# Unsplit float32 second products for every second chunk of block 1 in an attention and two-layer MoE kernel

## The chip, the core and the metric

The kernel runs on one core of one Trainium2 chip. The metric is the device time of one execution in microseconds (us). Engines are named as in the profile: PE is TensorE, PEld its weight loads, DVE is VectorE, ACT is ScalarE, POOL is GpSimd, SP is SyncE.

## What is computed

Attention over 1536 tokens (2 batches of 768, 8 heads of 64) with a window and block sums, then a dense feed-forward layer, then a layer of 8 experts with one expert per token. The change is in the dense layer, with 1536 tokens, a width of 512 and a hidden width of 2048:

```python
def _moe_ref(x, w_in, w_out):
    h = x @ w_in
    g = np.where(h > 0.0, h, np.exp(np.minimum(h, 0.0)) - 1.0)
    return (g @ w_out).astype(np.float32)

# reference: x = attention(q, k, v); x = _moe_ref(x, ...); return _moe2_ref(x, ...)
```

`g @ w_out` is called the second product here.

## The kernel before

The tokens are handled in four blocks of 512, 256, 384 and 384 tokens (`UNITS` = 8, 4, 6, 6 units of 64); block 1 is the second one, with two tiles of 128 tokens. The hidden width is cut into 16 chunks of 128. The first part of the program, `part1`, goes through 64 steps (block j, chunk c). In step i it issues, in this order: `mm_h` (the first product of chunk c, 12 matmuls into a PSUM bank h, of which there are two), `split_w` for the same chunk, `split_g` for the chunk of the step before, `elu` (three ACT operations, L432 to L434, and two DVE operations, L435 and L436, which leave g in the tile elp), and `mm_y` for the chunk of two steps before, which adds into the block's banks y, one for each tile of 128 tokens. Beside these, the steps carry the attention of the later blocks (`scores` L308, `turn` L370, `weighted` L391 and what belongs to them), and, in the first steps of a block, the logits of the block before (`lg1` and `lg2`, L499 to L525).

Full float32 precision is reached in two ways. Split: a float32 number is cut into a high part in the type fp32r and the remainder, and a product is made of three matmuls (high with high, high with low, low with high). For the second product this takes two operations for the weights of a chunk (`split_w`: an ACT cast at L174 and a DVE subtraction at L175, into the tile wsp) and two for g (`split_g`: L446 on ACT into gh, L447 on DVE into gl). Unsplit: one matmul instruction on the float32 tiles as they are, with weights straight from the tile wo and g from elp. Before the change the first eight chunks of block 0 are unsplit (`C3` = 8).

elp of a split chunk lies in a pool of two buffers with the tag p. gh and gl have two buffers each; an unsplit chunk of block 0 puts its elp into one of theirs, odd chunks under the tag gh, even ones under gl.

The order on each engine in `part1` is not that of the code: a scheduler with a timeline of its own places the instructions, except in the start-up, whose order is a hand-written table. The second part (routing of the last block and the experts) is ordered by a planner with fixed costs; it contains no second product of block 1.

Of the kernel before, what the change touches and what calls it, by code (L numbers as in the profile page):

```python
# [35 lines left out]
BLK = [j for j in range(NBLK) for _ in range(UNITS[j])]  # L36
NF = FF // 128
NS = 6
C3 = 8
WARM = 22  # L40
AT0 = (2, -2, 1)
ATS = (5, 4, 5)
# [36 lines left out]
class Prog:  # L79
# [86 lines left out]
            self.conv_l(c)  # L166

    def split_w(self, j, c):
        if j == 0 and c < C3:
            return  # L170
        nc = self.nc
        f = self.w[c, 1].bitcast(F32)
        w = self.ws.tile([128, 2, 512], F32R, tag="ws", name="wsp")
        nc.scalar.copy(w[:, 0], f)  # L174
        nc.vector.tensor_tensor(w[:, 1], f, w[:, 0].bitcast(F32), op=ALU.subtract)  # L175
        self.wsp[j, c] = w
# [247 lines left out]
    def elu(self, j, c):  # L424
        nc = self.nc
        h = self.h.pop((j, c))
        t = self.el.tile([128, TB], F32, tag="t", name="elt", bufs=1)[:, :TBS[j]]
        e = self.el.tile([128, TB], F32, tag="e", name="ele", bufs=1)[:, :TBS[j]]

        pool, tag = (self.gp, "gh" if c % 2 else "gl") if j == 0 and c < C3 else (self.el, "p")  # L430
        p = pool.tile([128, TB], F32, tag=tag, name="elp")[:, :TBS[j]]
        nc.scalar.activation(t, h, AF.Tanh, scale=0.5)  # L432
        nc.scalar.activation(e, h, AF.Exp)  # L433
        nc.scalar.activation(p, h, AF.Relu)  # L434
        nc.vector.scalar_tensor_tensor(t, e, 1.0, t, op0=ALU.add, op1=ALU.mult)  # L435
        nc.vector.scalar_tensor_tensor(p, t, 0.0, p, op0=ALU.min, op1=ALU.add)  # L436
        self.g[j, c] = p

    def split_g(self, j, c):
        nc = self.nc  # L440
        if j == 0 and c < C3:
            return
        p = self.g[j, c]
        gh = self.gp.tile([128, TB], F32R, tag="gh", name="gh")[:, :TBS[j]]
        gl = self.gp.tile([128, TB], F32R, tag="gl", name="gl")[:, :TBS[j]]
        nc.scalar.copy(gh, p)  # L446
        nc.vector.tensor_tensor(gl, p, gh.bitcast(F32), op=ALU.subtract)  # L447
        self.g[j, c] = (gh, gl)
# [7 lines left out]
    def mm_y1(self, j, c, t):  # L456
        nc = self.nc
        g = self.g[j, c]
        sl = slice(t * 128, t * 128 + 128)
        if j == 0 and c < C3:  # L460
            ops = ((g, self.w[c, 1].bitcast(F32)),)
        else:
            w = self.wsp[j, c]
            ops = ((g[0], w[:, 0]), (g[0], w[:, 1]), (g[1], w[:, 0]))
        for n, (gx, wx) in enumerate(ops):
            nc.tensor.matmul(self.y[j][t], lhsT=gx[:, sl], rhs=wx, start=(c == 0 and n == 0), stop=(c == NF - 1 and n == len(ops) - 1))  # L466
# [1032 lines left out]
```

## Time and profile before

| | |
|---|---|
| median of 3 runs | 552.49 us (551.38 to 555.17) |
| the profiled execution | 552.2 us, span of its instructions 550.4 us |
| PE busy | 528.4 us (96% of the span) |
| DVE, ACT, POOL busy | 357.8, 312.5, 74.2 us |
| mean granted clock of TensorE | 0.994 of full speed |

The profile is one execution. Busy times are shares of the span. Matmuls are pipelined, so the duration of a single one contains its drain; how much work PE gets through is read from the distance between the starts of consecutive matmuls.

### The profile page before, as it was taken

The numbers are of one execution on the slowest core, as the hardware profiler recorded it, in microseconds if no ns is written. First come the engines' busy times: TensorE is split into PE (matmuls) and PEld (weight loads), VectorE is DVE, ScalarE is ACT, GpSimd is POOL, SyncE is SP. The second block draws the span as 40 slices with busy tenths as digits, with TensorE's granted clock in tenths as the row PEclk, the third lists the DMA queues.
The fourth block names the chain that finished last, engine by engine and source line by source line (L and its number), as shares of the span: only waits on it lengthen the run. The fifth ranks groups of instructions, "written<-read, shape, count | busy, mean of one in ns | idle before, by whom it ended". The sixth has DMA issues, their size and how long they took to land. (4 is left out here: it accounts for less than half of the span.)

```text
span 550.4 us, 9589 instructions
## 1 busy us (share of the span) xinstructions
PE 528.4 (96%) x3113; PEld 417.6 (76%) x3113; DVE 357.8 (65%) x994; ACT 312.5 (57%) x768; POOL 74.2 (13%) x111
## 2 busy tenths in 40 slices
PE   7867999999998999999999999999999999999995
PEld 4456666688897888988888888978888575575883
DVE  6999899999557887786565789986631101444510
ACT  5875567767458786776665756662233232565620
POOL 3653000001000000000000001421421111100001
PEclk9999999999999999999999999999999999999998
DMA  9999843433114112211001004431286979594601
GB/s 296 315 359 403 269 155 105 151 99 95 53 56 153 49 50 80 69 49 49 2 0 59 1 1 130 120 96 57 67 299 243 393 255 358 156 381 140 236 21 42
DMA packets 38715, 81.34 MB, mean 148 GB/s; under 512 B 4095, under 2 KB 8575, under 8 KB 38656
## 3 DMA queue, kind: packets, MB, share of 16 engines
q1 hardware_dynamic: 36336, 73.30, 39.4%
q0 software_dynamic: 2320, 7.34, 3.8%
q8 instruction: 26, 0.43, 0.3%
q14 instruction: 33, 0.27, 0.1%
HBM read 103.70 MB, written 6.55 MB: 200 GB/s over the span
## 5 line engine op out<-in xcount | busy, mean ns | idle before, releaser
L421 PE MATMUL h<-xh,wi 128*128 128x384 f32 (+2 forms) x528 | 145.9, 343 | 0.5 <-ACT elp L434 0.5
L421 PEld LDWEIGHTS h<-xh,wi 128*128 128x128 f32 x528 | 94.0, 189 | 8.6 <-issue 1.0
L466 PE MATMUL y<-wsp,gh 128*128 128x512 f32 x320 | 98.5, 398 | 0.1
L421 PE MATMUL h<-xl,wi 128*128 128x384 f32 (+2 forms) x264 | 87.9, 333 | 0.0
L466 PEld LDWEIGHTS y<-wsp,gh 128*128 128x128 f32 x320 | 57.8, 188 | 10.1 <-ACT gh L446 0.6
L1157 DVE TENSOR_TENSOR holdl<-S,holdh 128x512 fp32r<-128x512 f32 x22 | 15.2, 689 | 72.5 <-ACT holdh L1153 53.7
L466 PE MATMUL y<-wsp,gl 128*128 128x512 f32 x160 | 60.5, 399 | 0.0
L1125 PE MATMUL h<-w2s,holdh 128*128 128x512 f32 x176 | 59.8, 400 | 0.0
L1168 PE MATMUL y<-w2s,holdh 128*128 128x512 f32 x176 | 59.0, 398 | 0.0
L421 PEld LDWEIGHTS h<-xl,wi 128*128 128x128 f32 x264 | 49.8, 189 | 4.6 <-issue 1.4
L435 DVE SCALAR_TENSOR_TENSOR elt<-ele,elt 128x384 f32<-128x384 f32 (+2 forms) x64 | 37.1, 580 | 23.8 <-ACT ele L433 23.5
L432 ACT ACTIVATE elt<-h 128x384 f32<-128x384 f32 (+2 forms) x64 | 31.3, 489 | 36.2 <-PE h L421 30.1
L175 DVE TENSOR_TENSOR wsp<-wo,wsp 128x512 fp32r<-128x512 f32 x56 | 39.2, 703 | 8.5 <-ACT wsp L174 8.0
L174 ACT CAST wsp<-wo 128x512 fp32r<-128x512 f32 x56 | 34.6, 621 | 15.6 <-PE y L466 13.1
L446 ACT CAST gh<-elp 128x384 fp32r<-128x384 f32 (+2 forms) x56 | 27.8, 497 | 21.8 <-DVE elp L436 14.7
L1168 PEld LDWEIGHTS y<-w2s,holdh 128*128 128x128 f32 x176 | 33.1, 188 | 8.4 <-issue 1.6
L1125 PEld LDWEIGHTS h<-w2s,holdh 128*128 128x128 f32 x176 | 33.1, 188 | 8.1 <-issue 0.8
L436 DVE SCALAR_TENSOR_TENSOR elp<-elt,elp 128x384 f32<-128x384 f32 (+2 forms) x64 | 35.5, 554 | 3.2
L335 ACT ACTIVATE e<-e,nb 128x120 f32<-128x120 f32 x88 | 33.7, 390 | 6.4 <-DVE nb L323 6.3
L447 DVE TENSOR_TENSOR gl<-elp,gh 128x384 fp32r<-128x384 f32 (+2 forms) x56 | 31.1, 555 | 7.6 <-ACT gh L446 7.6
L296 POOL COPY k<-ks 128x96 f32<-128x96 f32 x16 | 8.2, 516 | 199.3 <-PE S L308 137.6
L1168 PE MATMUL y<-w2s,holdl 128*128 128x512 f32 x88 | 34.4, 391 | 0.0
(291 smaller groups left out, 949.7 us busy)
## 6 DMA issues: line engine op xcount, KB each, us to landing
wo<-in_w SPq DMA_DIRECT2D x9, 2048.0 KB
wo<-in_w SPq DMA_DIRECT2D x18, 1024.0 KB
ri<-in_w_in SPq DMA_DIRECT2D x16, 512.0 KB
ro<-in_w_out SPq DMA_DIRECT2D x16, 512.0 KB
wo<-in_w SPq DMA_DIRECT2D x32, 256.0 KB
w2p<-in_w SPq DMA_DIRECT2D x32, 256.0 KB
w2q<-in_w SPq DMA_DIRECT2D x24, 256.0 KB
q<-in_q SPq DMA_DIRECT2D x18, 256.0 KB
```

The source lines that it names most:

```text
L174: nc.scalar.copy(w[:, 0], f)
L175: nc.vector.tensor_tensor(w[:, 1], f, w[:, 0].bitcast(F32), op=ALU.subtract)
L335: nc.scalar.activation(e[:, p], e[:, p], AF.Exp, bias=nb[:, p:p + 1], scale=0.125, accum_out=sm[:, p:p + 1])
L421: nc.tensor.matmul(h, lhsT=w[:, wl, k * 128:k * 128 + 128], rhs=x[:, k, a:b], start=(n == 0), stop=(n == 11))
L432: nc.scalar.activation(t, h, AF.Tanh, scale=0.5)
L435: nc.vector.scalar_tensor_tensor(t, e, 1.0, t, op0=ALU.add, op1=ALU.mult)
L436: nc.vector.scalar_tensor_tensor(p, t, 0.0, p, op0=ALU.min, op1=ALU.add)
L446: nc.scalar.copy(gh, p)
L447: nc.vector.tensor_tensor(gl, p, gh.bitcast(F32), op=ALU.subtract)
L466: nc.tensor.matmul(self.y[j][t], lhsT=gx[:, sl], rhs=wx, start=(c == 0 and n == 0), stop=(c == NF - 1 and n == len(ops) - 1))
L1125: nc.tensor.matmul(self.h[s, hf], lhsT=x[:, k], rhs=w, start=(n == 0), stop=(n == 11))
L1168: nc.tensor.matmul(self.y2[s], lhsT=g[:, ks], rhs=w, start=(i == 0 and n == 0), stop=(i == 7 and n == 2))
```

## The change

A set `WHOLE` of pairs (block, chunk) replaces the constant `C3`. It holds chunks 0 to 7 of block 0, as before, and the even chunks 0, 2, ... 14 of block 1. For these, `split_w` and `split_g` do nothing, `mm_y1` issues one float32 matmul for each tile in place of three, and `elu` puts elp into a buffer of gh or gl; in block 1 chunks 0, 4, 8 and 12 take gl, and 2, 6, 10 and 14 take gh.

```diff
-C3 = 8
+WHOLE = {(0, c) for c in range(8)} | {(1, c) for c in range(0, NF, 2)}
@@ split_w
-        if j == 0 and c < C3:
+        if (j, c) in WHOLE:
             return
@@ elu
-        pool, tag = (self.gp, "gh" if c % 2 else "gl") if j == 0 and c < C3 else (self.el, "p")
+        pool, tag = (self.gp, "gh" if (c >> j) % 2 else "gl") if (j, c) in WHOLE else (self.el, "p")
@@ split_g
-        if j == 0 and c < C3:
+        if (j, c) in WHOLE:
             return
@@ mm_y1
-        if j == 0 and c < C3:
+        if (j, c) in WHOLE:
             ops = ((g, self.w[c, 1].bitcast(F32)),)
```

The scheduler places everything around it anew. Three places show how. First PE where block 1's second products begin, right behind the first matmuls of block 0's logits (L524, on mab). y<-wsp,gh and y<-wsp,gl are split passes, y<-wo,elp is an unsplit product, "x2" is two instructions in a row. Before:

```order
L499 MATMUL y<-c_128,m 128x128 x4
L466 MATMUL y<-wsp,gh 128x512 x2
L466 MATMUL y<-wsp,gl 128x512
L466 MATMUL y<-wsp,gh 128x512 x2
L466 MATMUL y<-wsp,gl 128x512
L370 MATMUL T<-c_128,e 120x128 x4
L466 MATMUL y<-wsp,gh 128x512 x2
L466 MATMUL y<-wsp,gl 128x512
L466 MATMUL y<-wsp,gh 128x512 x2
L466 MATMUL y<-wsp,gl 128x512
L524 LDWEIGHTS mab
```

and in the change, at the same place:

```order
L499 MATMUL y<-c_128,m 128x128 x4
L466 MATMUL y<-wo,elp 128x512
L466 MATMUL y<-wsp,gh 128x512 x2
L466 MATMUL y<-wsp,gl 128x512
L466 MATMUL y<-wo,elp 128x512
L370 MATMUL T<-c_128,e 120x128 x4
L466 MATMUL y<-wo,elp 128x512
L466 MATMUL y<-wsp,gh 128x512 x2
L466 MATMUL y<-wsp,gl 128x512
L466 MATMUL y<-wo,elp 128x512
L524 LDWEIGHTS mab
```

Before, chunks 0 and 1 of one tile, then of the other, stand here; now chunks 0, 1 and 2 do, with 0 and 2 unsplit.

Second, PE in the middle of the block, at the end of the first product of chunk 10 (weights wi_1151) and the beginning of that of chunk 11 (wi_1200); between them stands the second product of chunk 8. Before:

```order
L391 MATMUL T<-et,v_98 64x64 x8
L308 MATMUL S<-k,q 128x120 x4
L421 MATMUL h<-xh_203,wi_1151 128x256
L421 MATMUL h<-xl_204,wi_1151 128x256
L421 MATMUL h<-xh_203,wi_1151 128x256
L466 MATMUL y<-wsp,gh 128x512 x2
L466 MATMUL y<-wsp,gl 128x512
L466 MATMUL y<-wsp,gh 128x512 x2
L466 MATMUL y<-wsp,gl 128x512
L421 MATMUL h<-xh_203,wi_1200 128x256
```

and in the change:

```order
L391 MATMUL T<-et,v_98 64x64 x8
L308 MATMUL S<-k,q 128x120 x4
L421 MATMUL h<-xh_203,wi_1151 128x256 x2
L421 MATMUL h<-xl_204,wi_1151 128x256
L421 MATMUL h<-xh_203,wi_1151 128x256
L466 MATMUL y<-wo,elp 128x512 x2
L421 MATMUL h<-xh_203,wi_1200 128x256
```

Six passes have become two instructions; the chunk's place, two steps behind its first product, is the same.

Third, ACT at the beginning of block 1, from the activations of chunk 0 to those of chunk 2. Before:

```order
L434 ACTIVATE elp<-h 128x256
L174 CAST wsp<-wo 128x512
L446 CAST gh<-elp 128x256
L236 COPY vs<-T 128x4x4
L432 ACTIVATE elt<-h 128x256
L433 ACTIVATE ele<-h 128x256
L434 ACTIVATE elp<-h 128x256
L236 COPY vs<-T 128x4x4
L446 CAST gh<-elp 128x256
L174 CAST wsp<-wo 128x512
L432 ACTIVATE elt<-h 128x256
```

and in the change:

```order
L434 ACTIVATE elp<-h 128x256
L174 CAST wsp<-wo 128x512
L236 COPY vs<-T 128x4x4
L432 ACTIVATE elt<-h 128x256
L433 ACTIVATE ele<-h 128x256
L434 ACTIVATE elp<-h 128x256
L446 CAST gh<-elp 128x256
L236 COPY vs<-T 128x4x4
L174 CAST wsp<-wo 128x512
L432 ACTIVATE elt<-h 128x256
```

The cast gh of chunk 0 is gone, and that of chunk 1 stands one place earlier. The orders of all engines are the same up to this place, but for names, and again from the middle of block 2 on.

## Rows read from the trace of the kernel before

**Rows 1.** Page, busy us of PE, and the granted clock in 40 slices

```profile
PE 528.4 (96%) x3113; PEld 417.6 (76%) x3113; DVE 357.8 (65%) x994; ACT 312.5 (57%) x768; POOL 74.2 (13%) x111
...
PEclk9999999999999999999999999999999999999998
```

**Rows 2.** Busy time by stretch; block 1 is 148.50:218.50

```profile
core 0: us, PE busy (x) PEld busy (x) DVE busy (x) ACT busy (x) POOL busy (x), PEclk, DMA share, GB/s
60.00:107.00 47.00, 47.00 (x216) 29.53 (x214) 42.96 (x107) 31.86 (x76) 0.27 (x1) 1.00 0.49 167
...
148.50:218.50 70.00, 68.62 (x556) 61.14 (x555) 51.38 (x181) 50.75 (x158) 2.20 (x7) 1.00 0.23 73
218.50:300.00 81.50, 81.50 (x531) 72.54 (x531) 54.62 (x161) 53.53 (x142) 1.08 (x3) 1.00 0.11 34
...
460.00:500.00 40.00, 40.00 (x194) 25.52 (x192) 16.28 (x26) 21.35 (x39) 4.41 (x4) 1.00 0.76 264
500.00:550.40 50.40, 43.60 (x204) 34.37 (x200) 13.13 (x21) 17.04 (x30) 4.91 (x5) 0.97 0.31 109
```

**Rows 3.** Timeline, ACT and PE around the wait: start us, us, engine, what

```profile
162.44 0.59 ACT L377 COPY et<-T 120x512 f32<-120x512 f32 x1 [0.93 <-PE T L370]
...
166.66 0.63 ACT L511 CAST mab<-y 128x512 bf16<-128x512 f32 x1
...
167.34 0.20 PE L524 MATMUL y<-wg,mab 128*128 128x48 bf16 x1 [1.38 <-ACT mab L511]
```

**Rows 4.** Groups by line, 148.5:218.5, DVE and ACT: busy us, mean ns, idle before

```profile
L175 DVE TENSOR_TENSOR wsp<-wo,wsp 128x512 fp32r<-128x512 f32 x16 | 11.0, 688 | 1.9 <-ACT wsp L174 1.7
L447 DVE TENSOR_TENSOR gl<-elp,gh 128x256 fp32r<-128x256 f32 x16 | 6.8, 426 | 2.2 <-ACT gh L446 2.2
...
L174 ACT CAST wsp<-wo 128x512 fp32r<-128x512 f32 x17 | 10.5, 620 | 4.2 <-PE y L466 4.2
...
L446 ACT CAST gh<-elp 128x256 fp32r<-128x256 f32 x16 | 6.5, 404 | 1.0 <-DVE elp L436 0.5 <-PE y L466 0.4
```

**Rows 5.** Groups by line and form, whole span, PE: all second products

```profile
L466 PE MATMUL y<-wsp,gh 128*128 128x512 f32 x320 | 98.5, 398 | 0.1
...
L466 PE MATMUL y<-wsp,gl 128*128 128x512 f32 x160 | 60.5, 399 | 0.0
...
L466 PE MATMUL y<-wo,elp 128*128 128x512 f32 x64 | 30.9, 622 | 2.5 <-DVE elp L436 2.5
```

**Rows 6.** Timeline, PE, an unsplit chunk of block 0

```profile
67.87 3.59 PE L466 MATMUL y<-wo,elp 128*128 128x512 f32 x8
70.90 0.79 PE L421 MATMUL h<-xh,wi 128*128 128x512 f32 x1
71.53 0.39 PE L421 MATMUL h<-xl,wi 128*128 128x512 f32 x1
```

**Rows 7.** Timeline, PE, two split chunks of block 1

```profile
196.03 0.63 PE L466 MATMUL y<-wsp,gh 128*128 128x512 f32 x2
...
197.41 0.28 PE L421 MATMUL h<-xh,wi 128*128 128x256 f32 x1
...
198.84 1.09 PE L466 MATMUL y<-wsp,gh 128*128 128x512 f32 x4
...
200.23 0.60 PE L370 MATMUL T<-c,e 128*120 128x128 f32 x4
```

**Rows 8.** Timeline, PE, from transposes back to split passes

```profile
200.59 0.37 PE L421 MATMUL h<-xh,wi 128*128 128x256 f32 x1
200.79 0.28 PE L421 MATMUL h<-xl,wi 128*128 128x256 f32 x1
200.91 0.40 PE L421 MATMUL h<-xh,wi 128*128 128x256 f32 x2
```

**Rows 9.** Timeline, ACT and PE at the beginning of block 1

```profile
149.48 0.39 ACT L434 ACTIVATE elp<-h 128x256 f32<-128x256 f32 x1
...
150.42 0.82 PE L308 MATMUL S<-k,q 128*128 128x120 f32 x6
...
152.07 0.17 ACT L236 COPY vs<-T 128x16 f32<-128x16 f32 x1 [0.53 <-PE T L235]
```

**Rows 10.** Timeline, chunk 1 of block 1, from h to elp

```profile
153.29 0.28 PE L421 MATMUL h<-xh,wi 128*128 128x256 f32 x1
...
154.83 0.43 DVE L436 SCALAR_TENSOR_TENSOR elp<-elt,elp 128x256 f32<-128x256 f32 x1
```

## The prediction, made before the changed kernel ran

> **What bounds the kernel now.** I read the busy shares first: TensorE (PE) is busy for 528.4 of 550.4 us, and its granted clock is at the upper level (2.4 GHz) in nearly every slice [rows 1]. An average says nothing about one stage, so the second view is busy time by stretch. Block 1, the one that the change touches, occupies PE from about 148.5 to 218.5 us. There PE is busy for 68.62 of 70.00 us, VectorE (DVE) for 51.38 and ScalarE (ACT) for 50.75 [rows 2]. So PE is the limit of this stage and the other two have over 18 us of slack each. The missing 1.38 us is one single wait of PE, for the part mab of block 0's logits, which ACT makes late [rows 3].
>
> Next comes what follows. From 218.5 to 300 us PE is busy for 81.50 of 81.50 us, from 460 to 500 us for 40.00 of 40.00 [rows 2]; only the tail after 500 us has larger holes. Whatever PE gains or loses in block 1 is therefore handed on: the work behind it already stands in an unbroken queue on PE. DVE and ACT time is worth something only where PE waits for it.
>
> **The removed work that is not on the path.** Eight chunks (c = 0, 2, ... 14) lose four instructions each: the two halves of the split of w_out (L174 on ACT, 0.620 us, L175 on DVE, 0.688 us) and the two of the split of g (L446 on ACT, 0.404 us, L447 on DVE, 0.426 us) [rows 4]. That is 8 x 1.024 = 8.2 us of ACT and 8 x 1.114 = 8.9 us of DVE. I cost all of it at nothing for the end time: both engines were idle for 18 us in this stretch, and PE waited for them 1.38 us in total. That is also the upper bound of what this relief can pay directly.
>
> Is even that 1.38 us freed? The wait ends with the ACT cast that starts at 166.66 us [rows 3]. In the order above, ACT's rows before that cast are those of before apart from one gh cast gone and a few casts moved, all of them before 160 us, and after them ACT runs dry: it waits 0.93 us for PE's transposes before the copy at 162.44 [rows 3]. What stands between that copy and the cast (copies of y, exponentials, xh) is unchanged. So the wait stays; I take 0 and keep -1.4 us as the end of the range.
>
> **The work on the path.** A split product of one 128-token tile is three PE passes (gh with w high, gh with w low, gl with w high). The unsplit product replaces these three by one instruction, which looks like a third of the work. The trace shows that it isn't. Block 0 already does c = 0 to 7 that way: 8 chunks x 4 tiles = 32 products, but the row on elp counts 64 matmuls [rows 5]. One float32 instruction is two records. In the timeline, eight such records start at 67.87 and the second matmul behind them starts at 71.53 [rows 6]. The first of those behind them takes one ordinary pass of 0.23 us, so the eight end at 71.53 - 0.23 = 71.30: 3.43 us, 0.43 us for a record and **0.858 us for a product**. The 0.59 us that rows show as a duration contains pipeline drain and must not be used.
>
> For the split form I read starts of consecutive work in block 1: a chunk's two tiles run from 196.03 to 197.41 us and another's from 198.84 to 200.23 us [rows 7], 1.38 and 1.39 us for six passes. That is 0.23 us a pass and **0.692 us for a product**. So each of the 16 products (8 chunks x 2 tiles) becomes 0.166 us longer: 16 x 0.166 = **+2.6 us on PE**.
>
> Weight loads add nothing of their own: they are inside these start-to-start distances in both forms. As the upper bound I keep the busy time of all 64 records, 30.9 us [rows 5], over 32 products: 0.966 us, drain and the first, slow batch included; that would be 16 x 0.274 = +4.4 us.
>
> The Trainium skill ("FP8 and Floating Point Precision", section "TensorE Precision Notes") says that true FP32 makes four passes through the array. With the trace's 0.23 us a pass that would be 0.92 us, and the sum +3.7 instead of +2.6 us; the trace's 0.858 us is a little under it and decides.
>
> **What the new order changes.** Where PE goes from a float32 transpose or score product to a split pass, it loses about 0.08 us: after the transposes, the matmul that starts at 200.59 is followed only at 200.79, 0.20 us later, where its neighbours follow at 0.12 us [rows 8]. Counted in the order of both kernels from the first score product of block 1 to the first h of block 2, such places (into a split or an unsplit matmul) fall from 17 to 14: 3 x 0.08 = -0.2 us. What the way back from a float32 product into split passes costs is already inside the 0.858 us, since [rows 6] is read past that switch. The remaining moves in block 2 exchange neighbours among work that was ready anyway; 0, with 0.3 us either way.
>
> **The waits that the buffers add.** elp of a whole chunk now lives in a buffer of tag gl or gh, so its Relu (L434) has to wait until an older part there has been read. In steady state that reader is the y product of three chunks earlier, which stands on PE ahead of the chunk's own h, so there is no wait. The start is different: chunk 0's elp takes the gl buffer of block 0's chunk 14, whose last pass ends as the next product starts at 150.42 us, while before its Relu began at 149.48 [rows 9]. ACT is held for about 1 us. Queued behind it stand one weight cast and the copy of vs, and that copy sat idle for 0.53 us until 152.07 anyway [rows 9]. Chunk 0's g is not read until after 167 us [rows 3]. Cost on PE: 0; bound above, 0.5 us, if the copy moved by the rest.
>
> **The sum.** +2.6 - 0.2 = +2.4 us. The profiled execution took 552.2 us with a span of 550.4, so it would become 554.6. The median of the runs shown is 552.49 us, 0.3 above the profiled one; I forecast **554.9 us**, a ratio of 1.004. About 1% (5.5 us) is what a measurement of this kernel can tell from no change, so this is a small loss inside that bound.
>
> **Rivals.**
> 1. *The relief pays after all.* The wait of 1.38 us goes, and block 1 loses most of its 17 switches. At most 2.6 - 1.4 - 17 x 0.08 = -0.2 us, so 552.3; the likely form (the wait alone) is 2.4 - 1.4 = +1.0, so 553.5. For it: 17 us of work leave the two engines. Against: the queue ahead of the cast is unchanged and PE has no other hole.
> 2. *The float32 product is as cheap as it looks:* one record of 0.43 us for a product. 16 x (0.43 - 0.692) = -4.2, so 548.3 us, faster than before. Against it stands the count of 64 records for 32 products, so I give it next to nothing.
> 3. *PE waits for elp.* The y product of a whole chunk now depends on Relu and two DVE operations directly. In chunk 1 of before, h ends at about 153.5 (last matmul at 153.29) and elp is ready at 154.83 + 0.43 = 155.26 us [rows 10], a chain of 1.8 us. What covers it: the order puts y(c-2), h(c+1), y(c-1) and h(c+2) between h(c) and y(c), 1.72 + 1.43 + 1.39 + 1.43 = 6.0 us (h from 197.41 to 198.84 in [rows 7]). It decides only if ACT's queue stretches the chain past 6.0 us; if it came to 7 us in all eight chunks, 8 x 1.0 us join: 562.9. Against it: block 0, with the same form, keeps PE busy for 47.00 of 47.00 us from 60 to 107 us [rows 2].
>
> **How the numbers follow.** Forecast 0.74, rival 1 0.13, rival 2 0.02, rival 3 0.07, and 0.04 for what I can't name, on both sides. The likeliest gives the time, 554.9. Below, the range takes rival 1's end, 552.3, and the 1.1 us by which the fastest run shown lies under the median (551.2), and above the upper bound of the product with one more wait of the size of the old one: 552.5 + 4.4 + 1.4 = 558.3, so 558.4. Faster by over 1% (under 547.0) is rival 2 with a lucky order: 0.03. Slower by over 1% (over 558.0) is rival 3 and a part of the unnamed: 0.10. The rest, 0.87, lies within 1%.
>
> **What would show it.** Right: the elp row of L466 counts 96 matmuls, gh 288 and gl 144; eight short stretches of block 1 with two products take 1.72 us each, start to start, against 1.39; the stretch from chunk 0's h to block 2's first h is about 72.4 instead of 70 us; busy PE rises by some 2.4 us while ACT falls by 8 and DVE by 9; the wait for mab is still there with 1.4 us; later stretches are the old ones, shifted. Wrong: a record count of 80 for elp (rival 2); a vanished mab wait (rival 1); idle time ahead of L466 rows with releaser L436 (rival 3); or PE holes behind 220 us that the table of stretches did not have.

## The result, and the profile after

| | before | after |
|---|---|---|
| median, timed side by side | 552.8 us (551.09 to 556.6) | 556.49 us (554.81 to 558.07) |
| profiled execution, span | 552.2, 550.4 us | 554.81, 553.0 us |

The ratio is 1.006, with a 95% interval of 1.0043 to 1.0077: the change costs 2.4 to 4.3 us. The forecast was 554.9 us, a ratio of 1.004, with 0.87 on "within 1%". The size, the sign and the place held; the forecast lies at the low end of the interval. It took about 1% as the least that can be told from no change; with 20 runs on each side the interval is 0.17% to either side, so this loss is told apart from none. Ratios, here and below, are of means, over the runs that lie at most 1.5% above the fastest of their kernel.

First the page after, the row that answers to [rows 1]:

```profile
PE 531.5 (96%) x3097; PEld 414.9 (75%) x3097; DVE 349.4 (63%) x978; ACT 306.4 (55%) x752; POOL 73.2 (13%) x111
```

PE gained 3.1 us of busy time while DVE lost 8.4 and ACT 6.1 (the rows of ACT that are gone lasted 8.2 us in all, but rows that follow each other overlap, and busy time counts an overlap once). Work left the two engines that had time and came to the one that had none.

The groups of the second product over the whole span, which answer to [rows 5] (busy us, mean ns | idle before):

```profile
L466 PE MATMUL y<-wsp,gh 128*128 128x512 f32 x288 | 90.8, 402 | 0.0
...
L466 PE MATMUL y<-wsp,gl 128*128 128x512 f32 x144 | 54.9, 398 | 0.0
...
L466 PE MATMUL y<-wo,elp 128*128 128x512 f32 x96 | 44.8, 594 | 2.5 <-DVE elp L436 2.5
```

16 products more without a split are 32 records more of elp (64 to 96), 32 fewer of gh and 16 fewer of gl. So a float32 matmul is two records in block 1 as well. And the only wait of all these rows for L436 is the old one of 2.5 us at the start of block 0.

Next the timeline of PE at one unsplit chunk of block 1, and at the logits (the second answers to [rows 3]):

```profile
178.34 1.88 PE L466 MATMUL y<-wo,elp 128*128 128x512 f32 x4
180.06 0.38 PE L370 MATMUL T<-c,e 128*120 128x128 f32 x2
```

```profile
166.58 0.20 PE L524 MATMUL y<-wg,mab 128*128 128x48 bf16 x1 [1.38 <-ACT mab L511]
```

Two products take 180.06 - 178.34 = 1.72 us, where the split form took 1.38 and 1.39 [rows 7]: 0.17 us more for each. The wait for mab has not changed by a hundredth.

Busy time by stretch, with the same columns as [rows 2]:

```profile
148.50:221.20 72.70, 71.32 (x541) 58.41 (x540) 46.21 (x168) 44.98 (x143) 1.60 (x6) 1.00 0.23 72
...
221.20:300.00 78.80, 78.80 (x516) 69.53 (x515) 51.92 (x156) 50.71 (x137) 0.95 (x3) 1.00 0.10 31
```

PE's only hole is still those 1.38 us, and behind block 1 it has none.

Where did the time go? One execution can't be compared by its span, because the clock differs in other places (last section). Two places of the program mark the stretch in which the orders differ: the transposes of vs at the beginning of block 1, and the first transposes of m in block 3 (from there on the orders are equal again). Before:

```profile
159.11 0.60 PE L242 MATMUL T<-c,vs 128*24 128x128 f32 x4
...
302.02 0.60 PE L499 MATMUL T<-c,m 128*128 128x128 f32 x4
```

After:

```profile
158.35 0.60 PE L242 MATMUL T<-c,vs 128*24 128x128 f32 x4
...
303.97 0.60 PE L499 MATMUL T<-c,m 128*128 128x128 f32 x4
```

That is 142.91 us before and 145.62 after: **+2.71 us**, against +2.4 in the forecast's sum. This distance, at an undisturbed clock of 1.00 and with the same work inside but for the second products that the edit changes, is the measure for the experiments on blocks 1 and 2 below; I call it the marked stretch.

### The profile page after: what moved, and what is told of

Read it like the earlier page. It is cut to its first block, busy times and chain, and to the rows that moved or that the text cites. A ratio compares the mean times of both kernels' runs of the same rounds, so it can differ in the third digit from the quotient of the medians.

```text
span 553.0 us, 9537 instructions
## 1 busy us (share of the span) xinstructions
PE 531.5 (96%) x3097; PEld 414.9 (75%) x3097; DVE 349.4 (63%) x978; ACT 306.4 (55%) x752; POOL 73.2 (13%) x111
## 5 line engine op out<-in xcount | busy, mean ns | idle before, releaser
L466 PE MATMUL y<-wsp,gh 128*128 128x512 f32 x288 | 90.8, 402 | 0.0
L1157 DVE TENSOR_TENSOR holdl<-S,holdh 128x512 fp32r<-128x512 f32 x22 | 15.2, 690 | 72.4 <-ACT holdh L1153 53.7
L466 PEld LDWEIGHTS y<-wsp,gh 128*128 128x128 f32 x288 | 52.3, 188 | 10.2 <-issue 1.4
L466 PE MATMUL y<-wsp,gl 128*128 128x512 f32 x144 | 54.9, 398 | 0.0
L466 PE MATMUL y<-wo,elp 128*128 128x512 f32 x96 | 44.8, 594 | 2.5 <-DVE elp L436 2.5
L175 DVE TENSOR_TENSOR wsp<-wo,wsp 128x512 fp32r<-128x512 f32 x48 | 33.7, 706 | 8.4 <-ACT wsp L174 7.9
L436 DVE SCALAR_TENSOR_TENSOR elp<-elt,elp 128x384 f32<-128x384 f32 (+2 forms) x64 | 35.5, 555 | 4.4 <-ACT elp L434 0.9
L174 ACT CAST wsp<-wo 128x512 fp32r<-128x512 f32 x48 | 29.6, 621 | 15.5 <-PE y L466 14.6
L446 ACT CAST gh<-elp 128x384 fp32r<-128x384 f32 (+2 forms) x48 | 24.6, 512 | 23.0 <-DVE elp L436 14.4
L1125 PE MATMUL h<-w2s,holdl 128*128 128x512 f32 x88 | 35.0, 398 | 0.0
```

The lines of the kernel that those rows point to most:

```text
L1125: nc.tensor.matmul(self.h[s, hf], lhsT=x[:, k], rhs=w, start=(n == 0), stop=(n == 11))
L1157: self.nc.vector.tensor_tensor(l, self.tx.pop((s, hf)), h.bitcast(F32), op=ALU.subtract)
```

## Experiments: how much for a product, and does the place matter

Four theories were to be told apart. A: a price for each product on PE. B: a loss from the new order or the buffers, whatever the number. C: the relief of ACT and DVE pays a part back. D, which came up on the way: in other places the work that a split product puts on ACT and DVE is what counts. The recorded expectations use letters of their own, explained in each of them, which don't always agree with these.

**All chunks of block 1 unsplit**, 32 products instead of 16:

```diff
-WHOLE = {(0, c) for c in range(8)} | {(1, c) for c in range(0, NF, 2)}
+WHOLE = {(j, c) for j, n in ((0, 8), (1, NF)) for c in range(n)}
```

> All 16 chunks of block 1 are unsplit, 32 products in place of 16, elp alternating between the buffers of gl and gh as in block 0. Theory A (only the length of the products on PE counts, 0.166 us each): +5.3 us less about 0.3 us of switches, about 557.8 us where before has 552.8, ratio 1.009. Theory B (the work taken off ScalarE and VectorE pays too, so that the loss flattens): twice the work is taken off, no wait for mab, ratio 1.006 or less. Theory C (each unsplit product costs what the end-to-end result says, 3.3 us over 16, because of something beside its length): +6.6 us, ratio 1.012. In the profile A shows the mab wait still there with about 1.4 us.

Measured: 556.96 us, ratio 1.0067 (1.0043 to 1.0091); the marked stretch is 4.18 us longer than before, so the second 16 products cost 1.47 us, about half of the first 16. The wait for mab is still there with 1.4 us, so it isn't the end of this wait that flattens the loss.

**A quarter of the chunks**, 0, 4, 8 and 12, with elp in a buffer of its own: 8 products.

```diff
+WHOLE = {(0, c) for c in range(8)} | {(1, c) for c in range(0, NF, 4)}
+        if j == 1 and c % 4 == 0:
+            p = self.el.tile([128, TBS[1]], F32, tag="pw", name="elp", bufs=1)
```

> Half the dose: only chunks 0, 4, 8 and 12 of block 1 are unsplit, 8 products in place of 16, and their elp lie in a buffer of their own. Theory A (a price per product on PE, 0.166 us): 8 x 0.166 = +1.3 us, ratio to the kernel before 1.0024; from the transposes of vs at the start of block 1 to block 3's first transposes of m the profile is 1.3 us longer (the change: +2.71, all 16 chunks: +4.18). Theory B (most of the loss is a fixed one, from the new order, whatever the number of products): about +2.7 us, 1.005. Theory C (the relief of ACT and DVE pays and is worth more the less PE has to bear): at or below 1.000.

Measured: 554.67 us, ratio 1.002 (0.9998 to 1.0042), which by itself can't be told from no change; the marked stretch is 1.03 us longer.

**Another place**: block 1 split again, and five chunks of block 2 with three tiles each unsplit, 15 products.

```diff
+WHOLE = {(0, c) for c in range(8)} | {(2, c) for c in range(1, NF, 3)}
```

> The same form in another place: block 1 all split as before, and in block 2 chunks 1, 4, 7, 10 and 13 unsplit, 5 chunks x 3 tiles = 15 products, their elp again in the buffers of gh and gl. Theory A (a price per product, wherever it stands): 15 x 0.166 = +2.5 us, ratio 1.0045. Rival (the loss belongs to block 1, to its start beside the logits of block 0 and the buffers there): 1.000 to 1.002 here.

Measured: 556.64 us, ratio 1.0063 (1.0041 to 1.0085). The two marks in this kernel, and the next transposes of m:

```profile
160.15 0.60 PE L242 MATMUL T<-c,vs 128*24 128x128 f32 x4
...
305.18 0.60 PE L499 MATMUL T<-c,m 128*128 128x128 f32 x4
...
310.08 0.60 PE L499 MATMUL T<-c,m 128*128 128x128 f32 x4
```

To the first transposes of m it is 2.12 us longer than before. But here these stand two matmuls of h earlier than in the other kernels, so the stretch holds less work. Up to the second transposes the work is the same again but for the 15 products; before, these were at

```profile
306.58 0.60 PE L499 MATMUL T<-c,m 128*128 128x128 f32 x4
```

That is 149.93 us against 147.47: 2.46 us longer.

| unsplit products more | 8 | 15 (block 2) | 16 (the change) | 32 |
|---|---|---|---|---|
| marked stretch, us longer | 1.03 | 2.46 (to the second transposes of m) | 2.71 | 4.18 |
| for a product | 0.13 | 0.16 | 0.17 | 0.13 |
| ratio | 1.002 | 1.0063 | 1.006 | 1.0067 |

The loss grows with the number of products and is there in block 2 as well. Theory B, a fixed loss that belongs to block 1, falls. The price in the stretch is 0.13 to 0.17 us. Two products in a row took 1.72 us in the kernel with 32 too, so their price is the same, and the other work of the stretch takes less time there. Fewer changes between kinds of matmul (37 places with 32 products, 41 before) explain 0.3 of the 1.1 us by which 32 products missed 32 x 0.166 = 5.3. Most of the rest is seen in `weighted` (L391): before, its matmuls stand in 16 runs, with 32 products in 13, and from the start of each run to the next work it is 8.19 us in all before and 7.53 with 32. A run cut in two is dearer than a whole one, here 0.61 + 0.26 us (before) against 0.61 (32 products):

```profile
171.45 0.68 PE L391 MATMUL T<-et,v 120*64 120x64 f32 x14
172.06 0.20 PE L524 MATMUL y<-wg,mab 128*128 128x48 bf16 x1
172.19 0.33 PE L391 MATMUL T<-et,v 120*64 120x64 f32 x2
172.45 1.21 PE L466 MATMUL y<-wsp,gh 128*128 128x512 f32 x4
```

```profile
176.76 0.69 PE L391 MATMUL T<-et,v 120*64 120x64 f32 x16
177.37 1.15 PE L308 MATMUL S<-k,q 128*128 128x120 f32 x8
```

So the loss is the price of the products less what the order around them gives back, in these four kernels 0 to 1.1 us. The two explanations overlap a little, and some 0.2 us stay open.

## Experiments: the relief and the buffers

**Relief alone, most of it.** The products stay split in three passes, but chunks 2, 4, ... 14 of block 1 take over the split parts of the chunk ahead of them, so the four operations of seven chunks are left out. Their products are then other numbers, tokens go to other experts, and nothing behind block 3 can be compared; the whole run (572.3 us) says nothing.

```diff
+LEND = {(1, c) for c in range(2, NF, 2)}
+        if (j, c) in LEND:
+            self.wsp[j, c] = self.wsp[j, c - 1]
+            return
@@ split_g
+        if (j, c) in LEND:
+            self.g[j, c] = self.g[j, c - 1]
```

> The kernel before, but chunks 2, 4, ... 14 of block 1 make no split parts of their own: their products, three passes each as before, read the parts of the chunk before them. So the split work of 7 chunks is left out (the output is not the reference's), and PE does as many passes as before. Theory A (relief of ScalarE and VectorE is worth nothing but a possible end of the one wait for mab): ratio 1.000, at best 0.9975 if that wait goes. Theory B (relief pays): ratio 0.995 or less, 2.8 us or more, in busy PE with fewer switches.

Measured: the marked stretch is 142.71 us, 0.20 shorter than before. The wait for mab nearly goes here, but another comes; the rows of PE's waits between 100 and 330 us (in total, times, longest) are

```profile
PE h L425 <- ACT elp L438: 0.6, 1, 0.6
PE y L531 <- ACT mab L518: 0.3, 1, 0.3
```

instead of one of 1.4 us (lines 421, 434, 511 and 524 stand at 425, 438, 518 and 531 here). In the new wait, at 167.61 us, a first product waits for an earlier chunk's Relu, which reads the bank h. So PE waits some 0.9 us where it waited 1.4, and 0.2 us come through: in the order that this kernel gets, the relief of both engines is worth 0.2 us in this block.

**DVE's relief, with the computation complete.** The weight subtraction of the even chunks moves to POOL; all products stay split.

```diff
-        nc.vector.tensor_tensor(w[:, 1], f, ...)
+        (nc.gpsimd if j == 1 and c % 2 == 0 else nc.vector).tensor_tensor(w[:, 1], f, ...)
```

> All products split as in the kernel before; the subtraction that makes the low part of the weights of block 1's even chunks goes from DVE to POOL, which takes 8 x 0.69 = 5.5 us off DVE and leaves PE's work alone. Theory A (the relief of DVE is worth nothing in block 1): ratio 1.000, within 0.001, and the stretch of PE as long as before. Rival (DVE's relief is worth something that the unsplit products' price hid): -1 us or more, 0.998 or less. A third way: POOL takes several us for one subtraction, wsp comes late, PE waits for it, over 1.002.

Measured: 553.64 us, ratio 1.0003 (0.9979 to 1.0026). The groups of POOL in block 1 show the moved work at twice its price on DVE (0.69 us), and no one waits for it:

```profile
L175 POOL TENSOR_TENSOR wsp<-wo,wsp 128x512 fp32r<-128x512 f32 x7 | 9.5, 1361 | 22.8 <-ACT wsp L174 22.8
```

The marked stretch changes by +0.16 us. Theory C falls by both runs, to within some 0.2 us.

**The price alone.** All split operations are kept, their results for the even chunks are just not read; the products are unsplit as in the change, and their elp lie in buffers of their own as in the next run. So the relief is left out.

```diff
-        self.g[j, c] = (gh, gl)
+        self.g[j, c] = p if (j, c) in BOTH else (gh, gl)
```

> The even chunks of block 1 take the unsplit product, but the split work of weights and g is still done for them, and its results are not read. elp of chunks 0, 4, 8, 12 has a buffer of its own. Theory A: the price alone, +2.6 us, the same as the changed kernel or up to 0.5 us more: ratio 1.004 to 1.006 against before. Theory B (relief was paying inside the changed kernel): more than the changed kernel, ratio 1.008 or above, with PE waiting for L436 or L446 in block 1.

Measured: 556.78 us, ratio 1.005 (1.0028 to 1.0072); marked stretch +3.02 us. With the same buffers and with the relief (the next run) it is +3.13 us: without any relief the change costs what it costs with it.

**Buffers of their own** for elp, in place of those of gh and gl:

```diff
-        p = pool.tile([128, TB], F32, tag=tag, name="elp")[:, :TBS[j]]
+        if j == 1 and c % 4 == 0:
+            p = self.el.tile([128, TBS[1]], F32, tag="pw", name="elp", bufs=1)
+        else:
+            p = pool.tile([128, TB], F32, tag=tag, name="elp")[:, :TBS[j]]
```

> The changed kernel with elp of block 1's chunks 0, 4, 8, 12 in a buffer of its own and of 2, 6, 10, 14 in the old buffers p, so that no part of gl or gh is held. Theory A (the buffers cost nothing: the wait of the Relu of chunk 0, 1.02 us on ScalarE in the changed kernel, hits nobody): the same as the changed kernel, ratio 1.004 to 1.006 against before. Theory D (sharing the buffers is the part of the loss above 2.4 us): 0.5 to 1 us less, ratio 1.004 or under.

Measured: 556.71 us, ratio 1.0054 (1.0028 to 1.008); marked stretch +3.13 us. In the change, ACT's Relu of chunk 0 does wait for the old reader of its buffer (ACT's timeline, after):

```profile
149.85 0.38 ACT L434 ACTIVATE elp<-h 128x256 f32<-128x256 f32 x1 [1.02 <-PE y L466]
150.13 0.61 ACT L174 CAST wsp<-wo 128x512 fp32r<-128x512 f32 x1
151.31 0.17 ACT L236 COPY vs<-T 128x16 f32<-128x16 f32 x1 [0.57 <-PE T L235]
```

The copy of vs behind it still waits 0.57 us for PE, as it did 0.53 [rows 9], so the 1.02 us of ACT were free. With own buffers the Relu's wait is gone,

```profile
151.97 0.39 ACT L437 ACTIVATE elp<-h 128x256 f32<-128x256 f32 x1
```

and the time is not shorter: sharing the buffers cost nothing. Of the 0.4 us by which this stretch is longer than in the change, 0.3 are a longer wait for mab (1.69 us).

## Experiments: the other direction, in block 0

If an unsplit product is dearer, fewer of the eight unsplit chunks of block 0 should make the kernel faster.

**Four of eight**, 16 products back to the split form:

```diff
-C3 = 8
+C3 = 4
```

> The other direction, in another block: block 1 as before the change, and in block 0 only chunks 0 to 3 unsplit in place of 0 to 7, so 16 products (4 chunks x 4 tiles) go from unsplit to split. Theory A (0.166 us a product on PE, and the split's other work is hidden): -2.7 us, ratio 0.995, and the wait-free stretch of PE in block 0 gets that much shorter. Theory D (there DVE decides: the split adds 4 x (0.69 + 0.69) = 5.5 us of DVE, more than the 4.0 us that it has free between 60 and 107 us): PE waits for wsp or gl in block 0, and the time stays the same or gets longer, 1.000 to 1.006.

Measured: 558.42 us, ratio 1.0079 (1.0049 to 1.0109). Theory A alone had 0.995; the rival, D, had 1.000 to 1.006, so the kind of loss was foreseen and its size was not. PE's waits from 60 us on, which before had one row (mab):

```profile
PE S L308 <- POOL k L296: 2.1, 1, 2.1
PE y L524 <- ACT mab L511: 1.5, 1, 1.5
PE h L421 <- ACT wi L151: 1.3, 2, 0.8
PE y L466 <- ACT wsp L174: 1.0, 1, 1.0
```

The new rows make 4.4 us, more than the 16 x 0.166 = 2.7 us saved, and behind the wait for k the granted clock is 0.50, the lower level, from 136 to 142 us.

**Six of eight**, 8 products back, `C3 = 6`:

> Block 1 as before the change; in block 0 chunks 6 and 7 become split too (unsplit: 0 to 5), 8 products in the other direction. PE is paid 8 x 0.166 = 1.3 us; DVE gets 2 x (0.68 + 0.69) = 2.7 us more, against the 4.0 us that were free between 60 and 107 us in the kernel before. Theory A with room on DVE: -1.3 us, ratio 0.9976, no new wait of PE. Theory D (DVE's queue up to 128 us, with the weight conversions in it, decides there): PE waits for wi, wsp or k appear as with four chunks, only smaller, and the ratio is 1.000 to 1.003.

Measured: 555.57 us, ratio 1.004 (1.0019 to 1.0061). From 107 to 128 us DVE was nearly full already in the kernel before (columns as in [rows 2]):

```profile
107.00:128.00 21.00, 21.00 (x108) 16.98 (x107) 20.16 (x38) 13.57 (x26) 2.26 (x2) 1.00 0.31 92
```

In the kernel with `C3 = 6`, PE waits 0.55 us for wsp at 118.65 and then for k at 130. Its timeline there, PE's row, POOL's, and the first and the last of seven DVE rows without a gap between them:

```profile
130.04 1.92 PE L308 MATMUL S<-k,q 128*128 128x120 f32 x8 [2.44 <-POOL k L296]
```

```profile
125.53 4.67 POOL L296 COPY k<-ks 128x96 f32<-128x96 f32 x2 [60.83 <-DVE ks L221]
```

```profile
125.56 0.68 DVE L447 TENSOR_TENSOR gl<-elp,gh 128x512 fp32r<-128x512 f32 x1
...
129.17 0.68 DVE L175 TENSOR_TENSOR wsp<-wo,wsp 128x512 fp32r<-128x512 f32 x1
```

Two copies of 128x96 take POOL 4.67 us, and end just behind DVE's dense run; before, the same two took

```profile
123.56 2.26 POOL L296 COPY k<-ks 128x96 f32<-128x96 f32 x2 [58.41 <-DVE ks L221]
```

and one alone takes 0.27 us where DVE rests (at 139.78 us in the kernel with `C3 = 6`). Behind PE's hole the granted clock is 0.56 and 0.59, the lower level, from 130 to 134 us (busy time by stretch, columns as in [rows 2]):

```profile
130.00:132.00 2.00, 1.96 (x9) 1.96 (x10) 0.01 (x1) 0.00 (x0) 0.19 (x1) 0.56 0.00 0
132.00:134.00 2.00, 2.00 (x6) 1.55 (x6) 2.00 (x10) 0.00 (x0) 0.27 (x1) 0.59 0.34 112
```

**With the weight subtraction on POOL**, for four and for two chunks less, to spare DVE:

```diff
+        (nc.gpsimd if j == 0 and c < 8 else nc.vector).tensor_tensor(w[:, 1], f, ...)
```

> Chunks 0 to 3 of block 0 unsplit in place of 0 to 7, as in the run that lost 0.8%, but the subtraction for the low part of the weights of chunks 4 to 7 runs on POOL, which is idle there: DVE gets 4 x 0.69 = 2.7 us more and not 5.5. If DVE's queue was what made that run slow, most of its loss goes: PE keeps its 16 x 0.166 = 2.7 us less, the waits for wi and wsp shrink below 1 us in total, and the ratio comes to 0.995 to 1.000. If it was ACT or the order around k, the ratio stays near 1.008.

> Chunks 0 to 5 of block 0 unsplit, and the subtraction for the weights of chunks 6 and 7 on POOL: 8 products fewer to pay on PE (-1.3 us), DVE 2 x 0.69 = 1.4 us more, well under the 4.0 us that it had free. Theory A with room: ratio 0.9976 and no new wait of PE. If the time doesn't fall although no new wait shows, the price per product is not 0.166 us in this place.

Measured: 558.76 us, ratio 1.0108 (1.0082 to 1.0134) with four chunks less. With two chunks less the median of all twelve runs is 558.97 us (550.85 to 560.17); the ratio, 1.0051 (1.0016 to 1.0087), is that of eight of them. Both expectations missed. With four chunks PE's largest wait is now

```profile
PE y L466 <- POOL wsp L175: 3.4, 1, 3.4
```

for a subtraction that took POOL 6.50 us beside a DVE without a gap:

```profile
90.46 6.50 POOL L175 TENSOR_TENSOR wsp<-wo,wsp 128x512 fp32r<-128x512 f32 x1 [7.25 <-ACT wsp L174]
```

With two chunks the subtractions took 1.30 and 1.36 us, but then the DVE operation that began beside each took 1.39 and 1.78 us instead of 0.68, and PE waits 2.3 us for the copies into k as without the edit. In both kernels POOL's work was held up by a full DVE or held DVE up, so moving more to it was the wrong cure.

**The copies taken off POOL.** `C3 = 6` again, and only the first two copies of block 2's summed keys move to ACT; the orders on PE and DVE are those of the run with `C3 = 6`.

```diff
-            self.nc.gpsimd.tensor_copy(k[:, 0], self.ks[u // UPB])
+            self.copy("A" if UPB <= u < UPB + 2 else "P", k[:, 0], self.ks[u // UPB])
```

> Chunks 0 to 5 of block 0 unsplit, block 1 all split, as in the run that lost 0.4%; the only other edit is that the first two copies of the summed keys into k for block 2's units go from POOL to ACT. The orders on PE and DVE are those of that run. There PE waited 2.4 us for the first of these copies at 130 us, and the granted clock fell behind the wait. Theory (POOL's copies, drawn out to 4.7 us for two while DVE runs without a hole, ate the gain): the wait of 2.4 us and the dip of the clock behind it go, only the 0.6 us for wsp stays, and the stretch from the first unsplit product to the transposes of vs is 105.5 to 106.2 us where it was 109.7 there and 106.6 in the kernel before; ratio 0.997 to 0.999. Rival (block 0 loses by something else, DVE's queue as a whole): the wait moves to wsp, wi or the copy on ACT, and the ratio stays at 1.003 to 1.004.

Measured: 553.43 us beside 553.49 for the kernel before, ratio 0.9999 (0.9976 to 1.0022). ACT does the two copies in 0.44 us, and PE's waits from 60 us on are

```profile
126.53 0.44 ACT L197 COPY k<-ks 128x96 f32<-128x96 f32 x2
```

```profile
PE y L524 <- ACT mab L511: 1.5, 1, 1.5
PE y L466 <- ACT wsp L174: 0.5, 1, 0.5
```

The wait for k and the fall of the clock are gone; from the first unsplit product to block 3's transposes of m the profile is 4.26 us shorter than with `C3 = 6` alone (54.02 to 301.22 against 53.33 to 304.79 us). That is the 2.44 us of the wait and 1.8 us more, put down to the lower clock: the split passes behind the wait start 0.43 us apart where the same passes start 0.23 apart in this run. Where two small copies run was the difference between 1.004 and 1.000. By the sum this kernel should be 8 x 0.166 - 0.5 = 0.8 us faster than the one before; between the same two marks, with the clock at 1.00 in both (249.55 - 1.62 = 247.93 us before, see the last section, and 247.20 here), it is 0.7. The times can't show that: the interval reaches 1.3 us to either side.

## Why the prediction was right, point by point

- *The bound.* PE was the limit of block 1 and stayed it. What was added to it reached block 3; the 8.2 and 8.9 us of work taken off ACT and DVE did not.
- *The price of a product.* 0.858 us from start-to-start distances in block 0 against 0.692 in block 1: confirmed by the two products in 1.72 us. One record of 0.43 us for a product would have given a gain of 4.2 us (rival 2).
- *The sum* was a little small: +2.4 forecast, +2.71 in the marked stretch, 2.4 to 4.3 by the times. Of its two terms the first, +2.6, is met by the 1.72 us. The second, -0.2 for fewer changes of kind, was counted to the first h of block 2 (17 to 14); over the whole stretch in which the order differs it is 41 to 39, so -0.16. It does not show: 16 products alone make 2.7 us, all of the 2.71 measured, so the rest of the stretch gave nothing back. In other kernels it did give something back (0.3 us with 8 products, 1.1 with 32), so that the sum came so close is in part luck.
- *A sign that did not come in the form I gave it.* The stretch from chunk 0's h to block 2's first h was to grow from 70 to 72.4 us. From the transposes of vs to that h it grew by 0.76 us only, because the border moved: 8 score matmuls (48 before, 40 after, of L308) and the last two gl passes now stand behind that h. At some 0.115 and 0.23 us each they are 0.9 + 0.5 us, which brings the 0.76 to 2.1; the rest up to 2.71 falls into block 2. A mark has to be a place on both sides of which the same work stands.
- *Rival 1, the relief pays*: wrong for block 1, by the relief without the price (-0.2 us) and the price without the relief (+3.02). The mab wait stayed as argued. But even where it fell to 0.3 us, a wait of 0.57 us came in another place and 0.2 us came through; my lower end of -1.4 was generous.
- *Rival 2, a cheap float32 product*: excluded by the 96 records and the 1.72 us.
- *Rival 3, PE waits for elp*: no row shows a wait for L436 in block 1. The buffers' wait on ACT was 1.02 us (about 1 forecast) and reached no one.

What the forecast did not ask, and the runs answered: the same trade has the other sign in block 0. There DVE is nearly full up to 128 us, and the split's operations delay wsp, wi and the copies to k until PE waits. The eight unsplit chunks of block 0 cost PE about 32 x 0.166 = 5 us; taking back two or four of them lost more than it gave in the kernel as it stands, and with the two copies on ACT taking back two was even. Taking back all eight was not run.

## What to carry to other kernels

Replacing several passes by one instruction is worth what the starts of the work behind it say, not its count or its row's duration: here one float32 matmul costs as much as 3.7 fp32r passes. Such a trade between a matrix engine and two elementwise engines is decided stage by stage; the busy table by stretch says which side is full, and the same edit that helps one block loses in the next. And work moved from one engine to a second can show up as the slowing of a third one beside it, so the first new wait in the chain is worth reading before the edit is called wrong.

## What the runs showed of the hardware

**A copy on POOL beside a busy DVE.** It took 0.27 us with DVE at rest; two took 2.26 us in the kernel before, 4.67 with two chunks more on DVE and 5.27 with four. The Trainium skill ("SBUF — State Buffer", section "Who interferes with whom") says that a DVE instruction with two inputs in SBUF and a POOL instruction that reads SBUF exclude each other, and that ACT never waits on anyone. The traces agree: the DVE rows beside the long copies are such two-input operations, and the same two copies took 0.44 us on ACT.

**The granted clock falls in some executions only, behind the same work.** After the wait of 2.5 us ahead of the first unsplit product the clock of the profiled execution before was 0.55, near the lower level, for 3 us (columns as in [rows 2]):

```profile
53.00:56.00 3.00, 3.00 (x5) 1.14 (x4) 3.00 (x7) 3.00 (x13) 0.00 (x0) 0.55 1.04 386
```

while after showed

```profile
53.00:56.00 3.00, 2.67 (x7) 1.27 (x8) 3.00 (x8) 2.73 (x10) 0.00 (x0) 1.00 1.03 406
```

behind a wait of 2.49 us. The same eight records, before and after:

```profile
52.47 5.28 PE L466 MATMUL y<-wo,elp 128*128 128x512 f32 x8 [2.48 <-DVE elp L436]
```

```profile
53.33 3.67 PE L466 MATMUL y<-wo,elp 128*128 128x512 f32 x8 [2.49 <-DVE elp L436]
```

It is worth 1.62 us: from there to the transposes of vs 106.64 us against 105.02, with the same work. Seven of the fourteen profiles of this document show the fall in this place, and the length of the wait doesn't tell which: behind 1.93 us it fell (32 products), behind 2.49 it didn't. Behind the 24 small matmuls of L530 it was the other way round: 1.00 in before, 0.50 in after,

```profile
374.00:377.00 3.00, 3.00 (x20) 2.60 (x19) 1.52 (x10) 0.22 (x1) 0.00 (x0) 1.00 0.12 46
377.00:380.00 3.00, 3.00 (x19) 2.42 (x18) 2.63 (x14) 0.80 (x2) 0.00 (x0) 1.00 0.00 0
```

```profile
377.00:380.00 3.00, 3.00 (x8) 2.32 (x7) 1.66 (x10) 0.43 (x2) 0.00 (x0) 0.50 0.00 0
```

which costs 1.5 us (eight passes in 3.47 us that took 1.93). Two such episodes, here or there, are about as large as the change itself. What decides whether one comes was not settled; for a difference of 3 us it means that spans of single executions can't be compared, and distances between marks at the same clock can.
